# Score-maximum pairs between the projections: visits of three slots, with the two row halves out of step

## The chip, the core and the metric

One core of a Trainium2 chip runs the whole kernel. The metric is the device time of one execution in microseconds (us); the median of three executions of the kernel before is 1766.52 us.

## What is computed

A transformer block with adaptive layer norm over 2048 rows of 512 elements, in float32. The part that matters here is the attention with 32 heads of 16 elements, and in it the softmax, whose row maximum the kernel finds ahead of the attention itself.

```python
q, k, v = qkv[0], qkv[1], qkv[2]            # from (h @ wqkv), 32 heads, Dh = 16
scores = jnp.einsum("bhqd,bhkd->bhqk", q, k) * scale
p = _softmax(scores, axis=-1)
o = jnp.einsum("bhqk,bhkd->bhqd", p, v)
...
x = x + ga * _A_ref(h, A_wqkv, A_wo)        # attention
h = _layernorm(x, axis=-1) * (1 + cb) + sb
x = x + gb * _B_ref(h, B_w1, B_b1, B_w2, B_b2)   # two-layer network with gelu
```

## The kernel before

The kernel writes the order of each engine's instructions out by hand (`manual_schedule`, L56): what the program emits first is what an engine executes first. Waits between engines follow from the tiles. PSUM has eight banks of 128 x 512 floats, and the kernel hands them out in fixed rings (L69 to L88): a product takes the next bank of its ring, and TensorE (PE) can write a bank only when the engine that reads the former product from it is done.

The program has four stages: norms and first projections (to about 92 us), the remaining projections (to about 301 us), the attention over 32 units of 4 heads and 512 query rows, and the network. This case is about the second.

*The projections.* `items` (L580) lists 34 of them: ten blocks of v and 24 of q and k. Each is a sum of twelve 128x128 by 128x512 products in one bank (`mm3`, L294: three terms, since each operand is split in a high and a low part), read by one copy on ScalarE (ACT; L316 or L361). `mm3` takes a list `fill` of functions and calls them spread evenly between its twelve products. With five, they fall behind products 3, 5, 8, 10 and 12.

*The pairs.* The softmax needs a bound on each row's maximum. For nine of the 32 units (`FRONT`, L36; `NU1` = 9) it is found in this stage, between the projections' products. The keys are held as sums and differences of two column blocks (`kpm`, built at L325 to L350), so that max(x, y) = (x + y)/2 + |x - y|/2: one product gives the differences ("V") and one the sums ("U"). `pair_slot` (L434) does one slot, which is V or U of pair n, for both row halves: a = 0 uses rows 0 to 47 of the array, a = 1 rows 64 to 111. A V slot ends in two absolute values on ACT, from PSUM to the SBUF tile `cp` (L454, six buffers). A U slot ends in two operations on VectorE (DVE; L458), each of which adds the product to its `cp` and takes the minimum along the row (signs are turned) into one column of `mxs`. Each is followed by a small read of the accumulator. There are 144 pairs, so 288 slots and 576 products, ACT operations and DVE operations in sum. When a unit is complete, `max_rows` (L462) reduces its columns on DVE, splits them on GpSimd (POOL), and one or two projections later transposes them on DVE and stores them by four DMAs; this goes through the list `todo`, of which each projection takes one entry (L636 to L638). `load_qm` (L392), called in V of every unit's third pair, loads the next unit's queries by six DMAs on SyncE's queue (SP).

*The order.* `slots` (L582 to L585) is V0, V1, V2, U0, V3, U1, ..., so that U of a pair stands five slots behind its V. `visit` (L589) does the next `VISIT` = 2 of them. From the seventh projection on (`FILL0` = 6), `fill` holds five visits, six in every seventh projection (L632): 144 in 28 projections. For this stage the pair products have a ring of six banks and the projections one of two (L572). After the stage the rings are dealt anew (L647), the keys of two more groups are loaded, and the attention begins.

Of the kernel before, what the change touches and what calls it, by code (L numbers as in the profile page):

```python
# [7 lines left out]
F32 = mybir.dt.float32  # L8
FR = mybir.dt.float32r
BF = mybir.dt.bfloat16  # L10
AF = mybir.ActivationFunctionType
ALU = mybir.AluOpType
# [4 lines left out]
P = 128  # L17
# [7 lines left out]
NB = 4  # L25
TB = S // NB
# [5 lines left out]
KR = 3 * DH  # L32
# [3 lines left out]
FRONT = (0, 1, 2, 3, 4, 5, 8, 6, 7, 9)  # L36
NU1 = len(FRONT) - 1
FILL0 = 6
VISIT = 2
OP0 = 1  # L40
OPN = 4
NWARM = 22
# [10 lines left out]
def block_kernel(ctx: ExitStack, tc: tile.TileContext, x, wqkv, wo, w1, b1, w2, b2, c, w_mod, out):  # L53
    nc = tc.nc
    te, ve, ac, gp, sy = nc.tensor, nc.vector, nc.scalar, nc.gpsimd, nc.sync
    ctx.enter_context(tc.manual_schedule())  # L56

    def pool(name, bufs=1, **kw):
        cm = tc.tile_pool(name=name, bufs=bufs, **kw)
        return cm, cm.__enter__()  # L60

    def close(cm):
        cm.__exit__(None, None, None)
# [10 lines left out]
    def ring(n):  # L74
        b = rings[n].pop(0)
        rings[n].append(b)
        return psum[b].tile([P, TB], F32, tag="b", name=n)

    def bank_mx():
        return ring("mx")  # L80

    def bank():
        return ring("sc")
# [35 lines left out]
    tcm, tpool = pool("tpool", bufs=2, side="right")  # L119
# [33 lines left out]
    def load_w(k):  # L153
        if k < 4:
            raw = tpool.tile([P, 2, KC, P], F32, tag="wraw", name="wraw")
            for w in (1, 0):
                sy.dma_start(raw[:, w], wq_r[:, :, w * D + k * P : w * D + (k + 1) * P])
        else:
            raw = vraw
            for i in range(KC):  # L160
                sy.dma_start(raw[:, i], wq_r[:, i, 2 * D :])
        raws[k] = raw
# [108 lines left out]
    def ln1(b):  # L271

        tiles = [x_tile(b, t) for t in range(4)]
        mv, rs = ln_stats(tiles)

        def rows():
            for t in range(4):
                ve.tensor_scalar(tiles[t], tiles[t], mv[:, t, 0:1], rs[:, t : t + 1],
                                 op0=ALU.subtract, op1=ALU.mult)
            return tiles  # L280

        return rows
# [84 lines left out]
    kst, kpm, qst, qmx = {}, {}, {}, {}  # L367
# [6 lines left out]
    def build_k(dst, src, g, t0=0, t1=S, parts=(0, 1, 2)):  # L374
        for i in parts:
            part = (0, 0, 1)[i]
            for a in range(2):
                r0 = a * 64 + i * DH
                sy.dma_start(dst[r0 : r0 + DH, :, t0:t1].bitcast(F32), heads(src, g, part, a, t0, t1))

    def load_k(g, tile):
        kst[g] = tile
        build_k(tile, qk_d[1][g // 2], g)

    def build_q(u, dst):
        g, qb = divmod(u, NB)
        for i, part in enumerate((0, 1, 0)):
            for a in range(2):
                r0 = a * 64 + i * DH
                sy.dma_start(dst[r0 : r0 + DH].bitcast(F32), heads(qk_d[0][g // 2], g, part, a, qb * TB, (qb + 1) * TB))  # L390

    def load_qm(u):  # L392

        qmx[u] = qmpool.tile([P, 2, TB], FR, tag="qmx", name="qmx", bufs=2)
        build_q(u, qmx[u])

    def load_q(u):

        qst[u] = qpool.tile([P, 2, TB], FR, tag="qst", name="qst", bufs=2)
        build_q(u, qst[u])  # L400
        if u in have:
            load_max(u)
# [9 lines left out]
    def one_rows(k):  # L412
        for a in range(2):
            r0 = a * 64 + KR
            sy.dma_start(k[r0 : r0 + 2].bitcast(F32), one_d[:, None, :].to_broadcast([2, 2, S]))

    mxs, left, vabs = {}, {}, {}
# [13 lines left out]
        ve.tensor_reduce(mxs[u][:, p, a, qc, kr : kr + 1], ps, axis=AX.X, op=ALU.max, negate=True)  # L431
        left[u] -= 1

    def pair_slot(kind, n):  # L434


        v, i = divmod(n, 16)
        u = FRONT[v]
        if u not in left:
            mxs[u] = small.tile([P, 2, 2, 4, 2], F32, tag="mxf", name="mxf")  # L440
            left[u] = 16
        r, p, qc = i // 8, (i // 4) % 2, i % 4
        t0 = (2 * r + (kind == "V")) * TB
        pss = [bank_mx() for _ in range(2)]
        for a, ps in enumerate(pss):
            rows = slice(a * 64, a * 64 + KR)
            te.matmul(ps, qmx[u][rows, p, qc * P : (qc + 1) * P], kpm[u // NB][rows, p, t0 : t0 + TB],  # L447
                      start=True, stop=True)
        if kind == "V" and i == 2:
            load_qm(FRONT[v + 1])  # L450
        if kind == "V":
            for a, ps in enumerate(pss):
                vabs[n, a] = tpool.tile([P, TB], F32, tag="cp", name="cp", bufs=6)
                ac.activation(vabs[n, a], ps, AF.Abs)  # L454
            return []
        for a, ps in enumerate(pss):
            v = vabs.pop((n, a))
            ve.tensor_tensor_reduce(v, ps, v, -0.5, 3.0e38, ALU.add, ALU.min, mxs[u][:, p, a, qc, r : r + 1])  # L458
        left[u] -= 1
        return [] if left[u] else [max_rows(u)]  # L460

    def max_rows(u):  # L462

        mn = small.tile([P, 2, 2, 4], F32, tag="mn", name="mn")
        ve.tensor_reduce(mn, mxs.pop(u), axis=AX.X, op=ALU.min)  # L465


        m2 = small.tile([P, 2, 16], FR, tag="m2", name="m2")
        mt = small.tile([P, 32], F32, tag="mt", name="mt")
        mf = mn.rearrange("p b a c -> p (b a c)")  # L470
        gp.tensor_copy(m2[:, 0], mf)  # L471
        gp.tensor_tensor(m2[:, 1], mf, m2[:, 0].bitcast(F32), op=ALU.subtract)

        def rest():
            ve.transpose(mt, m2.rearrange("p s j -> p (s j)").bitcast(F32))
            for b in range(4):
                q0 = b * 32
                sy.dma_start(m_d[u][:, :, q0 : q0 + 32].rearrange("s j q -> (s j) q"), mt[q0 : q0 + 32])
            have.add(u)
            if u in qst:  # L480
                load_max(u)

        return rest
# [30 lines left out]
    ps = bank()  # L514
# [10 lines left out]
    rest = lambda: None  # L525
# [8 lines left out]
    for b in range(NB):  # L534
# [7 lines left out]
        if b + 1 < NB:  # L542
            rows = ln1(b + 1)
# [32 lines left out]
    def load_v(g):  # L576
        vg[g] = vgpool.tile([P, NKC, VG], F32, tag="vg", name="vg")
        sy.dma_start(vg[g], v_d[:, :, g])

    items = [(None, b, t) for b, t in vitems] + [(k, b, w) for k in range(1, 4) for b in range(NB) for w in (1, 0)]  # L580
    nv = len(vitems)
    slots = [("V", 0), ("V", 1)]  # L582
    for n in range(2, 16 * NU1):
        slots += [("V", n), ("U", n - 2)]
    slots += [("U", 16 * NU1 - n) for n in (2, 1)]  # L585
    led, todo = 0, []
    new = []

    def visit():  # L589
        nonlocal led  # L590
        for sl in slots[led : led + VISIT]:
            new.extend(pair_slot(*sl))
        led += VISIT

    for n, (k, b, w) in enumerate(items):
        if n == 1:
            close(acm)
            st[0] = sy
        if n < 3:
            build_k(kts[0], kpm_d[0], 0, 2 * TB, S, (n,))  # L600
        if n == 8:
            build_k(kts[1], kpm_d[0], 1)
            for t in kts:
                one_rows(t)
        if n == nv + 1:
            close(vwcm)
            kqcm, kqpool = pool("kqpool")
            kq = [kqpool.tile([P, 2, S], FR, name="kq0")]
            one_rows(kq[0])
            vgcm, vgpool = pool("vgpool", bufs=2)  # L610
            qcm, qpool = pool("qpool")
        if n == nv + 2:
            load_k(0, kq[0])
        if n == nv + 10:
            kpm[2] = kts[0]
            build_k(kts[0], kpm_d[1], 2)
        if n == nv + 15:
            load_v(0)
        if n == nv + 19:
            load_k(2, kts[0])  # L620
        if n == nv + 18:
            load_q(0)
        if n == nv + 20:
            load_q(1)
        if k and b == 1 and w and k < 3:
            split_w(k + 1)
            if k + 2 < 4:
                load_w(k + 2)
        new = []
        fill = [rest]  # L630
        if n >= FILL0:
            fill = [lambda rest=rest: (rest(), visit())] + [visit] * (4 + (n % 7 == 0))  # L632
        if n == len(items) - 1:
            fill += [lambda: None] * 2
        rest = proj_qk(b, k, w, fill) if k else proj_v(b, w, fill)
        for f in todo[:1]:  # L636
            f()
        todo = todo[1:] + new  # L638
    rest()
    while led < len(slots):  # L640
        new = []
        visit()
        todo += new
# [219 lines left out]
    for s in range(NS):  # L863
        u, kc = divmod(s, NKC)
# [3 lines left out]
        new = []  # L868
# [156 lines left out]
```

## Time and profile before

| | |
|---|---|
| median of three executions | 1766.52 us (1766.45 to 1767.83) |
| the profiled execution, its own time | 1765.35 us |
| its span, first to last instruction | 1763.6 us |
| granted TensorE clock, mean | 0.998 |
| first pair product | 92.2 us |
| last pair product starts | 300.0 us |
| first product of the attention | 301.20 us |

The profile is of one execution. Times of the timeline count from the first instruction. A row of the timeline gives the start, the length, the engine, the line of the kernel, the operation, what it writes from what, and how many such instructions in a row were joined; "PEld" is TensorE loading weights, which has its own row and can overlap the products. A bracket at its end gives the engine's idle time before it and what ended it. The length of a product holds the time in the array's pipeline, so that the distance between the starts of two bursts tells more than the busy time.

### The profile page before, as it was taken

The page shows a single profiled execution, that of the slowest core. Times are in us where ns is not written, and L with a number is a line of the kernel's source. Part 1 is how long each engine was busy: PE and PEld are TensorE (multiplying, and loading weights), DVE is VectorE, ACT ScalarE, POOL GpSimd, SP SyncE. Part 2 cuts the span into 40 slices and gives each one's busy share as a digit, 9 for nine tenths or more (in the row PEclk, how much of TensorE's full clock was granted, in tenths as well). Part 3 has the DMA queues.
Part 4 walks back from the last instruction along what each step waited for, and adds up shares of the span by engine and source line. Part 5 has one row for each costly group of instructions (what it writes and reads, how often), then busy time and mean ns, then how long its engine had stood idle before and what let it go on. Part 6 is the DMA issues. An engine that isn't in the chain of part 4 may idle for free.

```text
span 1763.6 us, 29164 instructions
## 1 busy us (share of the span) xinstructions
PE 1748.7 (99%) x10554; PEld 901.1 (51%) x10554; DVE 1404.5 (80%) x2553; ACT 1355.8 (77%) x2580; POOL 320.1 (18%) x347
## 2 busy tenths in 40 slices
PE   8999999999999999999999999999999999999998
PEld 6755555344343443343343343343433478788887
DVE  6579999898888888888888888888886286838453
ACT  3478888999999999999999999999999732213222
POOL 3204422010000000000000000000003154636462
PEclk9999999999999999999999999999999999999999
DMA  8767636811500411411410101101013064423341
GB/s 277 250 141 163 151 115 130 130 37 29 87 23 23 82 27 23 74 36 23 74 35 24 38 25 33 38 23 36 23 60 104 22 195 131 126 78 114 102 120 48
DMA packets 124100, 144.17 MB, mean 82 GB/s; under 512 B 38930, under 2 KB 72722, under 8 KB 122004
## 3 DMA queue, kind: packets, MB, share of 16 engines
q1 hardware_dynamic: 120644, 135.55, 30.9%
q10 hardware_dynamic: 3312, 6.76, 1.0%
q8 instruction: 83, 1.36, 0.3%
q14 instruction: 61, 0.50, 0.1%
HBM read 106.37 MB, written 35.87 MB: 81 GB/s over the span
## 4 chain that ended last, share of the span: by engine, by line
PE 93%; DVE 3%; DMA 1%; issue 1%; POOL 1%; SPq 0%; ACT 0%; ACTq 0%; DVEq 0%; POOLq 0%
PE pv L693 29%; PE mx L429 19%; PE sc L300 16%; PE sc L860 13%; PE mx L447 6%; PE mx L924 5%; PE pv L924 2%; PE sc L800 1%; PE mx L800 1%; DMA wmod<-in_w_mod_dram 1%; DVE glo L907 0%; POOL w2l L731 0%; DMA rb<-rden 0%; PE sc L257 0%; DVE mxs L431 0%
## 5 line engine op out<-in xcount | busy, mean ns | idle before, releaser
L861 ACT ACTIVATE p<-sc 128x512 f32<-128x512 f32 x2048 | 1054.8, 615 | 39.4 <-PE sc L860 13.4
L431 DVE TENSOR_REDUCE mxs<-mx 128x1 f32<-128x512 f32 x1472 | 927.5, 684 | 112.9 <-PE sc L860 76.6
L693 PE MATMUL pv<-p,vg 128*32 128x512 f32 x4096 | 546.0, 605 | 0.0
L860 PE MATMUL sc<-qst,kq 50*128 50x512 f32 x1024 | 284.1, 435 | 0.0
L860 PE MATMUL sc<-qst,kt 50*128 50x512 f32 x1024 | 282.3, 431 | 0.0
L429 PE MATMUL mx<-kq,qmx 48*128 48x512 f32 x768 | 262.1, 428 | 0.2
L429 PE MATMUL mx<-kt,qmx 48*128 48x512 f32 x704 | 240.3, 428 | 0.1
L429 PEld LDWEIGHTS mx<-kq,qmx 48*128 48x128 f32 x768 | 122.6, 184 | 228.5 <-DVE mxs L431 209.2
L903 ACT ACTIVATE g<-sc,b_c 128x512 f32<-128x512 f32 x56 | 38.6, 690 | 237.2 <-PE sc L300 233.1
L429 PEld LDWEIGHTS mx<-kt,qmx 48*128 48x128 f32 x704 | 113.3, 184 | 208.8 <-DVE mxs L431 191.1
L458 DVE CUSTOM_DVE_ANT_0 cp<-mx,cp 128x512 f32<-128x512 f32 x288 | 187.2, 688 | 36.3 <-PE mx L447 31.3
L471 POOL CAST m<-mn 128x16 fp32r<-128x16 f32 x32 | 6.3, 197 | 1026.0 <-DVE mn L465 1026.0
L454 ACT ACTIVATE cp<-mx 128x512 f32<-128x512 f32 x288 | 156.3, 597 | 38.8 <-PE mx L447 38.4
L693 PEld LDWEIGHTS pv<-p,vg 128*32 128x32 f32 x4096 | 81.1, 108 | 180.7 <-issue 169.3
L860 PEld LDWEIGHTS sc<-qst,kq 50*128 50x128 f32 x1024 | 125.5, 185 | 32.1 <-ACT p L861 23.6
L907 DVE TENSOR_TENSOR glo<-g,ghi 128x512 fp32r<-128x512 f32 x56 | 60.1, 1073 | 94.8 <-ACT ghi L906 94.8
L860 PEld LDWEIGHTS sc<-qst,kt 50*128 50x128 f32 x1024 | 125.5, 185 | 10.1 <-ACT p L861 3.1
L447 PE MATMUL mx<-kt,qmx 48*128 48x512 f32 x576 | 113.4, 455 | 0.0
L729 POOL TENSOR_TENSOR w1l<-w1r,w1h 128x512 fp32r<-128x512 f32 x56 | 76.8, 1372 | 152.7 <-DVE w1h L728 130.5
L447 PEld LDWEIGHTS mx<-kt,qmx 48*128 48x128 f32 x576 | 58.3, 184 | 56.4 <-issue 33.4
L300 PE MATMUL sc<-hThi,w 128*128 128x512 f32 x256 | 84.0, 436 | 2.2 <-DVE hThi L263 2.2
L731 POOL TENSOR_TENSOR w2l<-w2r,w2h 128x512 fp32r<-128x512 f32 x56 | 81.1, 1448 | 6.6 <-DVE w2h L730 6.2
(158 smaller groups left out, 1671.4 us busy)
## 6 DMA issues: line engine op xcount, KB each, us to landing
w1r<-in_B_w_dram SPq DMA_DIRECT2D x56, 256.0 KB
w2r<-in_B_w_dram SPq DMA_DIRECT2D x56, 256.0 KB
qk<-parts SPq DMA_DIRECT2D x25, 512.0 KB
qmx<-qk SPq DMA_DIRECT2D x192, 64.0 KB
qst<-qk SPq DMA_DIRECT2D x192, 64.0 KB
wmod<-in_w_mod_dram SPq DMA_DIRECT2D x6, 1024.0 KB
kq<-qk SPq DMA_DIRECT2D x24, 256.0 KB
kt<-qk SPq DMA_DIRECT2D x24, 256.0 KB
```

The costliest lines, as they stand in the source:

```text
L300: te.matmul(ps, p, q, start=i == 0, stop=i == len(terms) - 1)
L429: te.matmul(ps, qmx[u][rows, p, qc * P : (qc + 1) * P], kst[u // NB][rows, p, kr * TB : (kr + 1) * TB], start=True, stop=True)
L431: ve.tensor_reduce(mxs[u][:, p, a, qc, kr : kr + 1], ps, axis=AX.X, op=ALU.max, negate=True)
L447: te.matmul(ps, qmx[u][rows, p, qc * P : (qc + 1) * P], kpm[u // NB][rows, p, t0 : t0 + TB], start=True, stop=True)
L454: ac.activation(vabs[n, a], ps, AF.Abs)
L458: ve.tensor_tensor_reduce(v, ps, v, -0.5, 3.0e38, ALU.add, ALU.min, mxs[u][:, p, a, qc, r : r + 1])
L693: te.matmul(cur_pv[0][32 * j : 32 * (j + 1)], vg[g][:, kc, j * VW : j * VW + 32], pt.pop((s, j)), start=kc == 0, stop=kc == NKC - 1)
L729: gp.tensor_tensor(alo, a, ahi.bitcast(F32), op=ALU.subtract)
L731: gp.tensor_tensor(blo, b, bhi.bitcast(F32), op=ALU.subtract)
L860: te.matmul(ps, k[r0 : r0 + KX, p, kc * P : (kc + 1) * P], q[r0 : r0 + KX, p], start=True, stop=True)
L861: ac.activation(pb, ps, AF.Exp, scale=SCALE)
L924: te.matmul(acc[qb][t], p[:, sl], q, start=f == 0 and n == 0, stop=f == NF - 1 and n == 2)
```

## The change

`VISIT` becomes 3. The list of slots is first written for one row half (`half`: V0, nothing, V1, U0, V2, U1, ..., nothing, U143), 290 entries. U of a pair stands three entries behind its V. The other half (a = 1) follows the same list one entry later. So in a slot one half does V while the other does U, and each slot gives one operation to ACT and one to DVE; at three of the 291 slots only one half has work. `half_slot` is `pair_slot` for one half. The products, the operations on ACT and DVE, the buffers and the rings are the same. The 97 visits are spread over the 28 projections, three in 15 of them and four in 13; in the last projection two empty entries are added to `fill`, as before.

```diff
-VISIT = 2
+VISIT = 3
...
-    def pair_slot(kind, n):
+    def half_slot(kind, n, a):
...
-            left[u] = 16
+            left[u] = 32
         r, p, qc = i // 8, (i // 4) % 2, i % 4
         t0 = (2 * r + (kind == "V")) * TB
-        pss = [bank_mx() for _ in range(2)]
-        for a, ps in enumerate(pss):
-            rows = slice(a * 64, a * 64 + KR)
-            te.matmul(ps, qmx[u][rows, p, qc * P : (qc + 1) * P], kpm[u // NB][rows, p, t0 : t0 + TB],
-                      start=True, stop=True)
-        if kind == "V" and i == 2:
-            load_qm(FRONT[v + 1])
+        rows = slice(a * 64, a * 64 + KR)
+        ps = bank_mx()
+        te.matmul(ps, qmx[u][rows, p, qc * P : (qc + 1) * P], kpm[u // NB][rows, p, t0 : t0 + TB],
+                  start=True, stop=True)
         if kind == "V":
-            for a, ps in enumerate(pss):
-                vabs[n, a] = tpool.tile([P, TB], F32, tag="cp", name="cp", bufs=6)
-                ac.activation(vabs[n, a], ps, AF.Abs)
+            if i == 2 and a == 0:
+                load_qm(FRONT[v + 1])
+            vabs[n, a] = tpool.tile([P, TB], F32, tag="cp", name="cp", bufs=6)
+            ac.activation(vabs[n, a], ps, AF.Abs)
             return []
-        for a, ps in enumerate(pss):
-            v = vabs.pop((n, a))
-            ve.tensor_tensor_reduce(v, ps, v, -0.5, 3.0e38, ALU.add, ALU.min, mxs[u][:, p, a, qc, r : r + 1])
+        v = vabs.pop((n, a))
+        ve.tensor_tensor_reduce(v, ps, v, -0.5, 3.0e38, ALU.add, ALU.min, mxs[u][:, p, a, qc, r : r + 1])
         left[u] -= 1
...
-    slots = [("V", 0), ("V", 1)]
-    for n in range(2, 16 * NU1):
-        slots += [("V", n), ("U", n - 2)]
-    slots += [("U", 16 * NU1 - n) for n in (2, 1)]
+
+    half = [("V", 0), None]
+    for n in range(1, 16 * NU1):
+        half += [("V", n), ("U", n - 1)]
+    half += [None, ("U", 16 * NU1 - 1)]
+    slots = list(zip(half + [None], [None] + half))
+    visits = -(-len(slots) // VISIT)
...
         for sl in slots[led : led + VISIT]:
-            new.extend(pair_slot(*sl))
+            for a in range(2):
+                if sl[a]:
+                    new.extend(half_slot(*sl[a], a))
...
-            fill = [lambda rest=rest: (rest(), visit())] + [visit] * (4 + (n % 7 == 0))
+            m, nm = n - FILL0, len(items) - FILL0
+            fill = [lambda rest=rest: (rest(), visit())] + [visit] * (visits * (m + 1) // nm - visits * m // nm - 1)
```

## The prediction

> **What bounds the kernel now.** I read first the page's totals and its chain of waits, then the stage that the change touches.
>
> ```profile
> span 1763.6 us, 29164 instructions
> PE 1748.7 (99%) x10554; PEld 901.1 (51%) x10554; DVE 1404.5 (80%) x2553; ACT 1355.8 (77%) x2580; POOL 320.1 (18%) x347
> ...
> PE 93%; DVE 3%; DMA 1%; issue 1%; POOL 1%; SPq 0%; ACT 0%; ACTq 0%; DVEq 0%; POOLq 0%
> PE pv L693 29%; PE mx L429 19%; PE sc L300 16%; PE sc L860 13%; PE mx L447 6%; PE mx L924 5%; PE pv L924 2%; PE sc L800 1%; PE mx L800 1%; DMA wmod<-in_w_mod_dram 1%; DVE glo L907 0%; POOL w2l L731 0%; DMA rb<-rden 0%; PE sc L257 0%; DVE mxs L431 0%
> ```
>
> PE carries 93% of the chain, and the pair products (L447) and projections (L300) are on it. So a microsecond that PE saves in their stage should be saved at the end, unless another engine takes over there. The stage's limits, from the line's own record, the first instruction of the attention behind it, and busy times by stretch (PE, weight loads, DVE, ACT, POOL, clock, DMA share, GB/s):
>
> ```profile
> L447 PE MATMUL mx<-kt,qmx x576: 383/492/503, 92.2 to 300.0; 48*128 48x512 f32 x192
> ```
>
> ```profile
> 301.20 0.72 PE L860 MATMUL sc<-qst,kq 50*128 50x512 f32 x3
> ```
>
> ```profile
> 150.00:200.00 50.00, 50.00 (x219) 26.35 (x218) 45.71 (x143) 40.92 (x77) 24.52 (x29) 1.00 0.49 162
> 200.00:250.00 50.00, 50.00 (x221) 26.24 (x220) 45.50 (x143) 40.35 (x77) 15.70 (x21) 1.00 0.56 131
> ```
>
> The stage lasts from 92.2 to 301.2: 209.0 us. PE is called busy throughout, DVE for 91% (45.5 of 50), ACT for 81%. A PE "busy" at 100% says little, since the record of a matmul holds its waiting too; what it does with the time is in the starts of its bursts (start, length, engine, line, count):
>
> ```profile
> 84.90 1.09 PE L300 MATMUL sc<-wv,hTlo 128*128 128x512 f32 x4
> 85.84 2.03 PE L300 MATMUL sc<-wv,hThi 128*128 128x512 f32 x8
> ...
> 182.47 0.73 PE L447 MATMUL mx<-kt,qmx 48*128 48x512 f32 x4
> 183.00 1.09 ACT L454 ACTIVATE cp<-mx 128x512 f32<-128x512 f32 x2
> 183.13 0.73 PE L300 MATMUL sc<-hThi,w 128*128 128x512 f32 x2
> 183.24 0.69 DVE L458 CUSTOM_DVE_ANT_0 cp<-mx,cp 128x512 f32<-128x512 f32 x1 [0.26 <-PE mx L447]
> 183.79 0.84 PE L447 MATMUL mx<-kt,qmx 48*128 48x512 f32 x4
> 183.85 0.09 DVE L458 DVE_READ_ACCUMULATOR2_ANT mxf<- 128x1 f32 x1
> 183.85 0.69 DVE L458 CUSTOM_DVE_ANT_0 cp<-mx,cp 128x512 f32<-128x512 f32 x1
> 184.32 1.09 ACT L454 ACTIVATE cp<-mx 128x512 f32<-128x512 f32 x2 [0.23 <-PE mx L447]
> 184.56 0.97 PE L300 MATMUL sc<-hThi,w 128*128 128x512 f32 x3
> 185.46 0.73 PE L447 MATMUL mx<-kt,qmx 48*128 48x512 f32 x4
> 186.12 0.73 PE L300 MATMUL sc<-hTlo,w 128*128 128x512 f32 x2
> ```
>
> Projections alone start every 0.235 us (84.90 to 85.84, four of them). Between pair products, a burst of two takes 0.66 (183.13 to 183.79) and one of three 0.89 (184.56 to 185.45). So a burst of n costs 0.19 + 0.235 n: each change between the 128-row products and the 48-row pairs costs 0.19 beyond the matmuls. The four pair products of a visit take 0.66 too (182.47 to 183.13): the two of a slot, on different row halves, run together, and a slot counts as one position. One visit in two takes 0.77 (183.79 to 184.56): 0.11 of waiting.
>
> By this count the stage now has 144 visits of two positions (144 x 0.66 = 95.0) and, inside the window, 144 projection bursts with 333 matmuls (144 x 0.19 + 333 x 0.235 = 105.6): 200.6. The other 8.4 of the 209.0 are about 76 waits of 0.11. ACT explains them: in the visit at 182.47 its two Abs end at 183.00 + 1.09 = 184.09, and the second position of the visit at 183.79, which takes over their two banks, would start at 183.79 + 0.33 = 184.12 with its weight load ahead of that.
>
> **The change, part by part.** *Fewer, longer visits.* 291 slots make 97 visits of three, three in 15 of the 28 projections and four in 13. 47 visits fewer save 47 x 2 x 0.19 = 17.9. Three half slots at the ends stand alone, so 291 positions replace 288 (0.7 more). A burst of three positions was never run here; I take 0.19 + 3 x 0.235 = 0.895, as for three projections; its upper bound is 1.00, with the 0.11 above. Counted out: 97 x 0.895 = 86.8 for the pairs; the gaps inside the window are 45 of four projections (1.13 each, 50.9), 48 of three (0.895, 43.0), and 4 of two in the last projection (0.66, 2.6). PE unhindered: 183.3, plus 0.2 since the first visit comes one matmul later.
>
> *Halves out of step.* Each slot now gives one Abs to ACT and one sum-and-minimum to DVE, instead of two to one of them by turns. The number of operations is unchanged. I read their prices from the groups of this stretch (busy time, then the mean ns of one) and, in the timeline, from two runs without a gap:
>
> ```profile
> L458 DVE CUSTOM_DVE_ANT_0 cp<-mx,cp 128x512 f32<-128x512 f32 x286 | 186.0, 688 | 36.3 <-PE mx L447 31.3
> L454 ACT ACTIVATE cp<-mx 128x512 f32<-128x512 f32 x288 | 156.3, 597 | 38.8 <-PE mx L447 38.4
> ...
> L316 ACT ACTIVATE raw<-sc 128x512 f32<-128x512 f32 x23 | 13.9, 604 | 0.0
> ...
> L475 DVE STREAM_TRANSPOSE mt<-m 128x32 f32<-128x32 f32 x8 | 1.6, 206 | 0.0
> ...
> L465 DVE TENSOR_REDUCE mn<-mxf 128x16 f32<-128x32 f32 x8 | 1.5, 186 | 0.3
> ```
>
> ```profile
> 92.75 4.09 ACT L454 ACTIVATE cp<-mx 128x512 f32<-128x512 f32 x8 [0.46 <-PE mx L447]
> ...
> 300.92 0.69 DVE L458 CUSTOM_DVE_ANT_0 cp<-mx,cp 128x512 f32<-128x512 f32 x1
> ...
> 301.53 0.69 DVE L458 CUSTOM_DVE_ANT_0 cp<-mx,cp 128x512 f32<-128x512 f32 x1
> ```
>
> Back to back, one DVE operation follows the other after 0.61 (300.92 to 301.53), though each lasts 0.69; an Abs after 0.51 (4.09 / 8). A visit of three thus needs 1.83 of DVE and 1.53 of ACT, against a PE period of 0.895 + 0.895 = 1.79 (gap of three) or 2.025 (gap of four). **This is where the gain meets its limit**: in the denser projections DVE is slower than PE.
>
> *The banks.* Six matmuls use up the ring of six, so every bank is wanted again exactly one visit later, and PE, which issues in order, stops at the first that isn't free. From a visit's start at 0: the first position's data are read from 0.53 (ACT in the rows: 182.47 to 183.00), DVE's third operation ends its accumulator read at 0.53 + 3 x 0.61 + 0.08 = 2.44. The next visit's third position starts 0.895 - 0.33 = 0.57 after that visit. With a gap of four it wants its bank at 2.025 + 0.57 = 2.60: free in time. With a gap of three at 1.79 + 0.57 = 2.36: 0.08 too early, and a late load costs the 0.11 besides, so a period of up to 1.98. DVE working without a pause gives 1.83; after a late visit the next is nearer to that. I take the middle, 1.91. In the last projection, with gaps of two, I take DVE's 1.83.
>
> Sum: 48 x 1.91 + 45 x 2.025 + 4 x 1.83 = 91.7 + 91.1 + 7.3 = 190.1. DVE's nine mn and mt jobs (0.19 + 0.21 each, 3.5 in all) sit beside PE work in the loose half, on the path in the tight half: 1.8. With the 0.2 above: 192.1 instead of 209.0, **16.9 us less**.
>
> *Cost nothing:* ACT's raw copy (0.60 once a projection) follows the three Abs of a visit and ends at 0.53 + 1.53 + 0.60 = 2.66; the next three end at 2.66 + 1.53 = 4.19, where with a gap of three their third bank is wanted at 1.79 + 2.36 = 4.15. DVE's operations end later than that anyway; uncovered, it is 0.04 + 0.11 in each of the 13 denser projections, 2.0, kept for the range. The waits behind the operations: U of a pair falls on the bank of its own V, six matmuls back, and V's cp buffer comes from the U whose bank it takes, so the bank waits of PE already cover both. The loads:
>
> ```profile
> 265.58 1.71 SPq L478 DMA_DIRECT2D m<-mt  x4
> 267.33 2.76 SPq L379 DMA_DIRECT2D kt<-qk  x6
> ...
> 286.72 3.88 SPq L390 DMA_DIRECT2D qmx<-qk  x6
> ```
>
> load_qm comes 28 slots before its first use: 28 x 0.73 = 20 us now (209.0 / 288), 28 x 0.66 = 18 then. The tail is the tight place: kt waits on SP behind the m stores at the end of the projection whose raw copy is the sixth from last, 36 us before the attention, and the qmx load for the attention is issued only at 286.72. After the change five projections remain from there: two with three visits (3 x 2.025 = 6.08), two with four (4 x 1.91 = 7.64) and the last (some 8): 35, nearly as long, so this chain isn't squeezed. Nothing behind the stage is altered; it moves forward whole.
>
> **The rivals.** *PE unhindered (1741):* if the third position's bank is free in time, because DVE starts sooner than 0.53 after a visit, the stage takes 183.5, 25.5 less. Against it: 1.83 of DVE in a period of 1.79, 52 times.
>
> *DVE sets the pace (1760):* if alternating waits keep the operations from following at 0.61, each costs 0.61 + 0.08 = 0.69: 288 x 0.69 + 3.5 = 202.2, 6.8 us less than before. For it: the custom operation's own record is 0.69. Against it: 300.92 to 301.53, and 183.24 to 183.85. The Trainium skill, in "TensorEngine Tiling (Array Packing)", section "PSUM Bottleneck", speaks for this one: packing the array speeds up the matmuls but not the emptying of PSUM, which then may become the bottleneck. By that rule alone the stage would stay at DVE's sum, as in this rival; the trace agrees as far as DVE's 91%, but leaves it 9%.
>
> *Six banks in one visit (slower, 1773 or more):* if the last release of a visit is needed earlier than in its third position, PE and DVE take turns. Needed at the second position, the period is 2.44 + 0.11 - 0.33 = 2.22, 97 x 2.22 = 215, 6 us more than before; at the first, 2.55 and 247, 38 us more. It decides at a mean period of 209 / 97 = 2.15. For it: no bank is spare any more. Against it: the bank order, worked out above, and weight loads that each wait for their own bank.
>
> *No change (1766.5):* if the stage's end hung on loads or POOL and not on PE. Against it: the attention's first matmul starts at the end of a PE burst, and its data's chain has slack.
>
> **How the numbers follow.** The profiled execution took 1765.35 (its span 1763.6); the median of three is 1766.52. 16.9 off that is **1749.6**. Chances: forecast 0.56 (its own range 1744 to 1757), unhindered 0.10, DVE's pace 0.22, no change 0.04, slower 0.08. Less than 0.2% (3.5 us) can't be told from no change. Faster 0.88, same 0.04, slower 0.08. The range 1743 to 1762 holds the forecast with the raw copy's 2.0, and DVE's pace with 2 us of start and end; it leaves out the slower rival, no change and the unhindered end.
>
> **What would show it.** Right: pair bursts "x6" of 0.9 to 1.0, 97 of them, the stage's end near 284.6, DVE above 95% busy in the stage, and PE's idle time before L447 ended by DVE's mxf rather than by "issue" in the projections with four visits, and hardly in those with three. The step on the switches is wrong if x6 bursts take over 1.1 in the loose projections; that on DVE, if operations without a wait follow at 0.69; that on banks, if the first or second weight load of a visit waits for DVE. The forecast is wrong if the attention begins after 294, or if it begins near 285 and the span doesn't shrink with it.

## The result and the profile after

The changed kernel takes 1751.04 us (median of four, 1749.52 to 1751.21) against 1766.49 (median of four, 1766.41 to 1767.83): a ratio of 0.9906, interval 0.9894 to 0.9918. That is 15.45 us less; 16.9 were forecast, and 1749.6 for the time.

The page of the changed kernel, its totals and the chain by engine:

```profile
span 1749.3 us, 28886 instructions
PE 1732.7 (99%) x10554; PEld 900.7 (51%) x10554; DVE 1396.8 (80%) x2553; ACT 1350.3 (77%) x2580; POOL 320.2 (18%) x347
...
PE 93%; DVE 3%; DMA 1%; issue 1%; POOL 1%; SPq 0%; ACT 0%; ACTq 0%; DVEq 0%; POOLq 0%
```

The same instructions are busy, 16 us less on PE, and the chain has the same shares: nothing new became the bound. The record of the pair products (now line 446) and, from the timeline, the first product of the attention:

```profile
L446 PE MATMUL mx<-kt,qmx x576: 383/425/502, 93.5 to 285.4; 48*128 48x512 f32 x192
```

```profile
286.83 0.50 PE L863 MATMUL sc<-qst,kq 50*128 50x512 f32 x2
```

The stage lasts from 93.45 to 286.83, 193.4 us instead of 209.0: **15.6 less**. Behind it 1462.4 us are left in both (1763.6 - 301.2 and 1749.3 - 286.8): all of it arrives at the end. Ahead of the stage the changed profile is 1.2 late, 0.2 of it because the first visit stands one product later; the rest arises in the first 24 us, where PE waits for the inputs. In the nine profiles of this study in which the visits start in the seventh projection, that start lies anywhere from 91.8 to 95.2, and what lies behind the stage lasts from 1460.9 to 1464.8 in all ten profiles, so that its equality here is partly chance. So below I compare the lengths of the stage, and single times only roughly; a time without an interval is that of one execution.

Busy times by stretch (columns as before):

```profile
150.00:200.00 50.00, 50.00 (x241) 28.51 (x238) 48.07 (x157) 42.46 (x82) 26.49 (x31) 1.00 0.61 171
200.00:250.00 50.00, 50.00 (x239) 28.30 (x236) 48.17 (x156) 42.51 (x82) 14.53 (x20) 1.00 0.53 142
```

DVE went from 91% to 96%, ACT from 81% to 85%. In the timeline, first a projection with three visits, then one with four:

```profile
184.37 1.20 PE L300 MATMUL sc<-hThi,w 128*128 128x512 f32 x4
185.50 0.98 PE L446 MATMUL mx<-kt,qmx 48*128 48x512 f32 x6
185.98 0.19 PEld L446 LDWEIGHTS mx<-kt,qmx 48*128 48x128 f32 x2 [0.19 <-DVE mxf L455]
186.41 1.19 PE L300 MATMUL sc<-hTlo,w 128*128 128x512 f32 x4
187.53 1.00 PE L446 MATMUL mx<-kt,qmx 48*128 48x512 f32 x6
...
196.63 0.96 PE L300 MATMUL sc<-hThi,w 128*128 128x512 f32 x3
196.78 0.69 DVE L455 CUSTOM_DVE_ANT_0 cp<-mx,cp 128x512 f32<-128x512 f32 x1
197.39 0.69 DVE L455 CUSTOM_DVE_ANT_0 cp<-mx,cp 128x512 f32<-128x512 f32 x1
197.53 1.11 PE L446 MATMUL mx<-kt,qmx 48*128 48x512 f32 x6
198.00 0.08 DVE L455 DVE_READ_ACCUMULATOR2_ANT mxf<- 128x1 f32 x1
198.14 0.19 PEld L446 LDWEIGHTS mx<-kt,qmx 48*128 48x128 f32 x2 [0.32 <-DVE mxf L455]
198.57 0.72 PE L300 MATMUL sc<-hThi,w 128*128 128x512 f32 x2
```

With gaps of four a visit takes 0.91 (185.50 to 186.41). With gaps of three it takes 1.04 (197.53 to 198.57): the weight loads of the third position, the last two of the six, start at 198.14, just after DVE's accumulator read of the visit before (198.00 + 0.08). That is the wait that the prediction priced, and it isn't the only such visit. Of the two weight loads of a third position, one takes over a bank that DVE empties; in all 48 visits behind a gap of three, this load starts 0.05 us after the end of DVE's accumulator read. Behind gaps of four, 39 of 43 follow within 0.1 too, but there they are late by little.

Over the whole stage, from the starts of the bursts (the gap is the number of projection products ahead of a visit; a visit lasts from its first product to the next projection product; without a wait that is 0.66 for two positions and 0.895 for three; the first visit and a few at the end of the stage are left out):

```
kernel              stage us  visits behind a gap of: 2          3          4
before               209.0    97 x 0.74   45 x 0.67   -
changed              193.4     3 x 1.28   48 x 1.06   44 x 0.93
halves out, two      202.1    97 x 0.66   43 x 0.66   -
halves in, three     219.0     4 x 1.53   44 x 1.36   47 x 1.20
one DVE op more      198.9     3 x 1.41   48 x 1.17   44 x 0.94
one ACT op more      193.3     3 x 1.28   48 x 1.07   44 x 0.93
from the fourth      197.3     3 x 1.26   12 x 1.06   80 x 0.93
gaps evened          194.9     -          55 x 1.12   40 x 0.90
```

### The profile page after: what moved, and what is told of

It is laid out like the page before. It is cut to its first block, busy times and chain, and to the rows that moved or that the text cites. A ratio compares the mean times of both kernels' runs of the same rounds, so it can differ in the third digit from the quotient of the medians.

```text
span 1749.3 us, 28886 instructions
## 1 busy us (share of the span) xinstructions
PE 1732.7 (99%) x10554; PEld 900.7 (51%) x10554; DVE 1396.8 (80%) x2553; ACT 1350.3 (77%) x2580; POOL 320.2 (18%) x347
## 4 chain that ended last, share of the span: by engine, by line
PE 93%; DVE 3%; DMA 1%; issue 1%; POOL 1%; SPq 0%; ACT 0%; ACTq 0%; DVEq 0%; POOLq 0%
PE pv L696 29%; PE mx L429 20%; PE sc L300 15%; PE sc L863 13%; PE mx L927 5%; PE mx L446 5%; PE pv L927 2%; PE sc L803 1%; PE mx L803 1%; DVE glo L910 0%; DMA wmod<-in_w_mod_dram 0%; POOL w2l L734 0%; DMA rb<-rden 0%; PE sc L257 0%; PE mx L257 0%
## 5 line engine op out<-in xcount | busy, mean ns | idle before, releaser
L429 PE MATMUL mx<-kt,qmx 48*128 48x512 f32 x704 | 240.0, 428 | 0.0
L429 PEld LDWEIGHTS mx<-kt,qmx 48*128 48x128 f32 x704 | 113.4, 184 | 208.4 <-DVE mxs L431 190.6
L455 DVE CUSTOM_DVE_ANT_0 cp<-mx,cp 128x512 f32<-128x512 f32 x288 | 182.5, 687 | 25.9 <-PE mx L446 23.2
L452 ACT ACTIVATE cp<-mx 128x512 f32<-128x512 f32 x288 | 151.6, 604 | 27.9 <-PE mx L446 27.0
L910 DVE TENSOR_TENSOR glo<-g,ghi 128x512 fp32r<-128x512 f32 x56 | 58.6, 1046 | 96.2 <-ACT ghi L909 96.2
L446 PE MATMUL mx<-kt,qmx 48*128 48x512 f32 x576 | 103.9, 442 | 0.1
L446 PEld LDWEIGHTS mx<-kt,qmx 48*128 48x128 f32 x576 | 54.6, 184 | 52.7 <-DVE mxf L455 26.4
L300 PE MATMUL sc<-hThi,w 128*128 128x512 f32 x256 | 77.7, 421 | 3.1 <-DVE hThi L263 3.1
```

Source lines behind the costliest of these rows:

```text
L300: te.matmul(ps, p, q, start=i == 0, stop=i == len(terms) - 1)
L429: te.matmul(ps, qmx[u][rows, p, qc * P : (qc + 1) * P], kst[u // NB][rows, p, kr * TB : (kr + 1) * TB], start=True, stop=True)
```

## The experiments

### The two halves of the change, each alone

The first keeps visits of two slots in the changed kernel:

```diff
-VISIT = 3
+VISIT = 2
```

> The changed kernel with visits of two slots (146 visits): the halves out of step alone. Theory (switches cost 0.19 each, and the waits of 0.11 of the kernel before come from ACT doing two Abs at once): no waits are left, 146 x 0.66 for the pairs and 146 x 0.19 + 333 x 0.235 for the projections, so the stage takes 202 to 204 us instead of 193.4 (changed) and 209.0 (before), and the time is 1760 to 1762. Rival 1, only the number of visits counts: the stage stays at 209 to 210 as before, 1767. Rival 2, only the step between the halves counts: 193, 1751.

It took 1759.76 us (ratio to before 0.9956, interval 0.9939 to 0.9972), just below the expected range, and its stage 202.1. In its timeline:

```profile
182.18 0.97 PE L300 MATMUL sc<-hThi,w 128*128 128x512 f32 x3
183.08 0.73 PE L446 MATMUL mx<-kt,qmx 48*128 48x512 f32 x4
183.74 0.73 PE L300 MATMUL sc<-hTlo,w 128*128 128x512 f32 x2
184.40 0.73 PE L446 MATMUL mx<-kt,qmx 48*128 48x512 f32 x4
185.06 0.73 PE L300 MATMUL sc<-hTlo,w 128*128 128x512 f32 x2
```

Every visit takes 0.66 (183.08 to 183.74, 184.40 to 185.06), behind gaps of three and of two alike: the waits of the kernel before are gone, and with them 6.9 us, with two visits more than before. Out-of-step halves are worth that much alone. The second puts visits of three into the kernel before, whose halves go in step:

```diff
-VISIT = 2
+VISIT = 3
...
+    visits = -(-len(slots) // VISIT)
...
-            fill = [lambda rest=rest: (rest(), visit())] + [visit] * (4 + (n % 7 == 0))
+            m, nm = n - FILL0, len(items) - FILL0
+            fill = [lambda rest=rest: (rest(), visit())] + [visit] * (visits * (m + 1) // nm - visits * m // nm - 1)
```

> The kernel before with visits of three slots (96 visits) in its own order, both halves in step: visits of V U V and U V U by turns. Theory (with six banks in one visit, DVE and ACT must share the work evenly): four operations of one engine come in one visit, DVE's last release falls at 0.53 + 4 x 0.61 + 0.08 = 3.05 or at 2.6, and the third position waits 0.4 and 0.8 by turns; mean period about 2.3, the stage 216 to 228 us, the time 1774 to 1786, slower than before. Rival, the number of visits alone counts: 193, 1751.

It took 1777.37 us, the stage 219.0: 10 us slower than before, although it changes between the products as seldom as the changed kernel does. Its timeline:

```profile
180.96 1.09 PE L447 MATMUL mx<-kt,qmx 48*128 48x512 f32 x6
181.98 0.96 PE L300 MATMUL sc<-hTlo,w 128*128 128x512 f32 x3
182.28 3.66 ACT L454 ACTIVATE cp<-mx 128x512 f32<-128x512 f32 x6 [0.78 <-DVE mxf L458]
182.87 1.70 PE L447 MATMUL mx<-kt,qmx 48*128 48x512 f32 x6
184.08 0.18 PEld L447 LDWEIGHTS mx<-kt,qmx 48*128 48x128 f32 x1 [0.35 <-DVE mxf L458]
184.51 1.20 PE L300 MATMUL sc<-hThi,w 128*128 128x512 f32 x4
```

One visit takes 1.02 (180.96 to 181.98), the next 1.64 (182.87 to 184.51): in it positions wait for DVE and ACT, which by turns get four operations in one visit. ACT itself stood idle 0.78 for DVE, since here an Abs also waits for a cp buffer. The view of waits counts these (total us, times, longest):

```profile
ACT cp L454 <- DVE mxf L458: 31.1, 42, 1.1
```

There is no such entry in the kernel before, nor in the changed one. How much of the loss comes from DVE and ACT getting four operations in one visit, and how much from the six cp buffers, this run doesn't tell; none was made with more buffers. Either way, the two halves of the change aren't a sum: alone they are worth -6.9 and +10.1, together -15.6.

### Which engine sets the pace in the dense projections

One unused operation more at the end of each visit, on DVE and, in another kernel with the same tile, on ACT (both lines are shown in one diff):

```diff
+    extra = const.tile([P, 64], F32, name="extra")
...
+        ve.tensor_reduce(extra[:, :1], ident, axis=AX.X, op=ALU.max)
         led += VISIT
...
+        ac.activation(extra, ident[:, :64], AF.Copy)
         led += VISIT
```

> The changed kernel with one operation more on DVE at the end of each visit (a maximum over 128 columns of a constant tile, about 0.2 us, its result unused). Theory (DVE's 3 x 0.61 set the pace in the projections with four visits, and have some 0.15 spare in those with three): the 52 visits behind gaps of three or two get longer by 0.17 to 0.21, the 45 behind gaps of four by 0 to 0.05: 9 to 13 us more, 1760 to 1764. Rival, ACT's three Abs or the latency of a bank set the pace: 0 to 3 us more, 1751 to 1754.

> The changed kernel with one operation more on ACT at the end of each visit (a copy of 64 columns of a constant tile, about 0.2 us, its result unused). Theory (DVE sets the pace, ACT has 0.2 spare at the third bank): 0 to 4 us more, 1751 to 1755. Rival, ACT sets the pace: 52 visits get longer by 0.15 to 0.2, 8 to 11 us more, 1759 to 1762.

On ACT it cost nothing: 1750.33 us, the stage 193.3. Its row in the groups (97 of 275 ns, 26.7 us of work that don't show in the time):

```profile
L596 ACT ACTIVATE extra<-ident 128x64 f32<-128x64 f32 x97 | 26.7, 275 | 0.0
```

On DVE the stage grew by 5.5 to 198.9: 0.10 in each visit behind a gap of three, 0.004 behind a gap of four. The time of 1760.00 lies in the expected range, but only 5.5 of its 9.0 more come from the stage (its profile begins the stage 1.7 late and has 1.7 more behind it), so the expected 9 to 13 were too many. DVE's own timeline says why:

```profile
186.14 0.68 DVE L456 CUSTOM_DVE_ANT_0 cp<-mx,cp 128x512 f32<-128x512 f32 x1
186.75 0.69 DVE L456 CUSTOM_DVE_ANT_0 cp<-mx,cp 128x512 f32<-128x512 f32 x1
187.36 0.69 DVE L456 CUSTOM_DVE_ANT_0 cp<-mx,cp 128x512 f32<-128x512 f32 x1
187.97 0.28 DVE L596 TENSOR_REDUCE extra<-ident 128x1 f32<-128x128 f32 x1
188.18 0.69 DVE L456 CUSTOM_DVE_ANT_0 cp<-mx,cp 128x512 f32<-128x512 f32 x1
```

With the extra operation DVE works without a pause, 2.04 a visit (186.14 to 188.18), and the period behind gaps of three is 0.895 + 1.17 = 2.06: now it is DVE's throughput. Without it the period is 1.96 and DVE's work 1.83: 0.13 of the 0.21 that the operation takes had been pause, the few mn and mt jobs aside. So in the changed kernel DVE's latency, the way from a visit's first products to the third release, sets the pace and not its throughput.

### Throughput or latency: even gaps

If DVE's throughput counted, it would help to alternate gaps of three and four, 1.90 on the average:

```diff
-            fill = [lambda rest=rest: (rest(), visit())] + [visit] * (visits * (m + 1) // nm - visits * m // nm - 1)
-        if n == len(items) - 1:
-            fill += [lambda: None] * 2
+            t = 12 * nm - 4
+            done = [min(visits, visits * (12 * m + i) // t) for i in range(13)]
+            fill = [lambda k=done[i + 1] - done[i], r=rest if not i else None: (r and r(), [visit() for _ in range(k)])
+                    for i in range(12)]
```

> The changed kernel with its 97 visits spread evenly over the products of all projections, so that gaps of three and four products alternate, instead of whole projections with gaps of three and others with gaps of four. Theory (a visit behind a gap of three is late because DVE's last release takes 2.44 us from the start of the visit before, whatever came ahead of that): some 50 gaps of three with 0.17 to 0.24 each as now, the stage 192 to 196 us, the time 1750 to 1754. Rival, DVE's throughput over several visits sets the pace (mean period 1.90 against 1.83): hardly any wait, the stage 184 to 188, the time 1742 to 1746.

It took 1753.42 us, the stage 194.9, so the rival fell. In the timeline a visit behind three projection products and one behind four:

```profile
179.80 0.97 PE L300 MATMUL sc<-hThi,w 128*128 128x512 f32 x3
180.70 1.25 PE L446 MATMUL mx<-kt,qmx 48*128 48x512 f32 x6
181.88 0.50 PE L300 MATMUL sc<-hThi,w 128*128 128x512 f32 x1
182.22 0.86 PE L300 MATMUL sc<-hTlo,w 128*128 128x512 f32 x3
183.00 0.99 PE L446 MATMUL mx<-kt,qmx 48*128 48x512 f32 x6
183.93 0.50 PE L300 MATMUL sc<-hTlo,w 128*128 128x512 f32 x1
```

1.18 and 0.93; over all, 55 x 1.12 and 40 x 0.90. A visit behind a gap of four is late by nothing. Of the 55 behind a gap of three, the 40 whose visit before stands behind a gap of four take 1.18 on the average (1.12 to 1.39), late by 0.28 (0.17 to 0.24 was expected), although DVE had stood idle for 0.22 on the average just before its work on the visit before. The 14 that directly follow another gap of three take 0.94: the visit before them is itself late, and its length gives DVE the time. What counts is the distance from one visit's start to the next visit's third position, and not the mean period.

### The length of a visit

```diff
-VISIT = 3
+VISIT = 1
```

> The changed kernel with visits of one slot (291 visits). Theory (each change between pair products and projection products costs 0.19): 291 x 0.425 + 291 x 0.19 + 332 x 0.235 = 257, the stage takes 254 to 258 us, the time is 1811 to 1816. Rival, the cost of a change is a constant of weight loads that overlap when bursts are short: the stage below 240, the time below 1798.

1818.67 us, the stage 259.3, both a little over the expected ranges (a position takes 0.430 instead of 0.425, 1.5 in all), and no overlap of short bursts. The timeline:

```profile
200.53 0.50 PE L446 MATMUL mx<-kt,qmx 48*128 48x512 f32 x2
200.97 0.49 PE L300 MATMUL sc<-hTlo,w 128*128 128x512 f32 x1
201.39 0.50 PE L446 MATMUL mx<-kt,qmx 48*128 48x512 f32 x2
201.82 0.49 PE L300 MATMUL sc<-hTlo,w 128*128 128x512 f32 x1
```

A burst of one position or of one product takes 0.42 to 0.44, which is 0.19 or 0.20 + 0.235. So the price of a change holds for bursts of one to four. The other way, visits of four on the ring of six:

```diff
-VISIT = 3
+VISIT = 4
```

> The changed kernel with visits of four slots (73 visits) on the same ring of six banks. Theory (a visit can't hold more slots than half the banks): the fourth position wants the first one's banks 0.8 after the visit's start, and DVE gives them back at 0.53 + 0.61 + 0.08 with 0.11 for the late load, 1.33 to 1.39: 73 x (1.13 + 0.55) + 332 x 0.235 + 73 x 0.19 = 215, the stage takes 208 to 220 us, the time is 1766 to 1778. Rival, fewer changes always win: 174 of PE, or DVE's 180, the time 1732 to 1740.

1775.49 us, the stage 216.5, slower than before. Its timeline:

```profile
181.43 0.96 PE L446 MATMUL mx<-kt,qmx 48*128 48x512 f32 x6
182.61 0.32 PEld L446 LDWEIGHTS mx<-kt,qmx 48*128 48x128 f32 x2 [0.65 <-ACT cp L452]
182.62 0.63 PE L446 MATMUL mx<-kt,qmx 48*128 48x512 f32 x2 [0.22 <-ACT cp L452]
183.18 1.18 PE L300 MATMUL sc<-hTlo,w 128*128 128x512 f32 x4
184.28 0.96 PE L446 MATMUL mx<-kt,qmx 48*128 48x512 f32 x6
```

The fourth position can't start before the first one's banks are free, 1.19 after the visit's start (181.43 to 182.62); a visit takes 1.75 instead of 1.13. In all 48 visits behind a gap of four, both weight loads of the fourth position start 0.05 after the release of their banks, one by ACT and one by DVE. Six banks hold three positions; a longer visit waits inside itself.

### A faster version

If only gaps of three cost something, the visits should have more products between them. They start three projections earlier:

```diff
-FILL0 = 6
+FILL0 = 3
```

> The changed kernel with the visits starting three projections earlier (in the fourth instead of the seventh): 97 visits over 31 projections, so that 27 have three visits and only 4 have four. Theory (waits of 0.17 behind a gap of three projection products, 0.04 behind a gap of four): 36 gaps change from three to four, 36 x 0.13 = 4.7 us less, 1745 to 1748. Rival, the waits belong to every visit whatever its gap: 1750 to 1752. Second rival, the keys' sums and differences, loaded during these projections, come too late for an earlier start: 1752 or more, with a wait of TensorE for a load in the first visits.

It took **1747.54 us** (median of four, 1746.95 to 1748.33; ratio to before 0.9894, interval 0.9878 to 0.9911), 3.5 less than the changed kernel. Its stage holds 36 more projection products (36 x 0.235 = 8.5), and 197.3 - 8.5 = 188.8 is 4.6 less than 193.4, as expected (4.7). Not all of it arrives in the time, since a wait ahead of the first visit lies outside this length. The second rival shows there, once:

```profile
86.98 1.02 PE L446 MATMUL mx<-kt,qmx 48*128 48x512 f32 x3 [0.93 <-DMA kt<-kpm]
```

The first visit waited 0.93 for the keys' load. A still earlier start, which was not run, should have little to win: 12 gaps of three are left, 12 x 0.13 = 1.6 by the same count.

## Why the prediction was right

*The price of a change between products, 0.19.* Right. 97 projection bursts took 96.2 in the changed kernel (96.5 counted), and bursts of one position, which were never run before, keep the price.

*A burst of three positions, 0.895.* Right: 0.90 behind gaps of four with even gaps.

*Why the kernel before waited.* Right. The 8.4 us of waits are gone when the halves go out of step; that run alone doesn't tell ACT from DVE, which then also gets its operations one by one. The trace of the kernel before does. In 94 of 96 visits behind a gap of two, the weight load of the fourth product starts 0.05 after the second Abs of the visit before has ended. In the 62 of them that take about 0.77 it starts 0.33 to 0.39 after the visit's start, in the others at most 0.25. For the visit at 183.79, where the prediction has this Abs end at 184.09, the load is:

```profile
184.14 0.18 PEld L447 LDWEIGHTS mx<-kt,qmx 48*128 48x128 f32 x1
```

*The third position, with gaps of three 0.12 on the average, with gaps of four nothing.* The place and the engine were right, the sizes a little small: 0.17 and 0.04. The latency itself was right: DVE's third release comes 2.45 at the least and 2.51 on the average after the start of a visit that a gap of three follows, against 2.44. But the step took the middle between DVE without pause (1.83) and a fresh start (1.98); measured is 1.96, near the latter. By terms: 48 x 0.05 = 2.4 and 44 x 0.037 = 1.6 more; the mn and mt jobs, priced at 1.8 by themselves, are contained in these waits; and the first and the last visit, in whose six slots (not three) only one half has work, hold three products each and take 0.66 instead of 0.895, 0.5 less. That leaves 1.7, and the stage is 1.5 longer than the 191.9 forecast beside the first visit's 0.2. That the total is so near is partly luck, since 4.0 too little for the waits and 2.3 too much elsewhere offset each other.

*Raw copies, cp buffers and loads at no cost.* Right: another 0.28 of ACT work a visit changes nothing, and the tail behind the stage is as long as before.

*The rivals.* PE unhindered would have been 183.5 for the stage, DVE at 0.69 each 202.2; 193.4 lies between, and operations that follow at 0.61 through a whole visit (186.14 to 187.97, with more work on DVE) refute the second. The Trainium skill's "TensorEngine Tiling (Array Packing)", section "PSUM Bottleneck", is borne out in a weaker form than in that rival: emptying PSUM does limit the denser gaps, by when it gives back a bank rather than by its sum (288 x 0.61 + 3.5 = 179). The section speaks of a fourfold speedup; here two products run together. The slower rival's point, a release needed before the third position, wasn't reached here, but in-step halves and visits of four, which wait at other positions too, are both slower than the kernel before.

*Three signs didn't come as written.* The stage's end was put near 284.6 (the sum gives 301.2 - 16.9 = 284.3) and came at 286.8; 1.0 lies ahead of the stage. Of "x6" bursts there are 95 instead of 97, and 62 are longer than 1.0, among them 47 of the 48 behind gaps of three. And the idle time before PE's weight loads was to be ended by DVE in the projections with four visits, and hardly in those with three. The view of waits doesn't separate them; in the changed kernel:

```profile
PEld mx L446 <- DVE mxf L455: 26.4, 84, 0.4
...
PEld mx L446 <- ACT cp L452: 17.1, 47, 0.4
PEld mx L446 <- issue: 4.7, 13, 0.4
```

131 of these 144 entries are put down to an engine. In the kernel before, which waited less, 90 went to "issue":

```profile
PEld mx L447 <- issue: 32.7, 90, 0.4
```

Yet 32.7 / 90 = 0.36 and 17.1 / 47 = 0.36: most entries are the idle time that follows any change of products. In the changed kernel all 97 bursts have one of 0.36 or 0.37 on the average ahead of their first load, under any of the names. Such a name says whose signal came last, not that it was late. Sorted by their place in the burst, the entries do separate: ahead of a third position's loads, 33 of the 48 visits behind gaps of three have one that DVE ended, and 11 of the 44 behind gaps of four. So the sign was right in kind, and its "hardly" too strong.

## What to carry to other kernels

Where two kinds of products alternate on PE, count the changes: here each costs as much as most of a product. How seldom one can change is set by the banks: a burst as long as the ring paid here with the work of the engines that empty it spread evenly through the burst, and lost with the halves in step; and then what counts is when the last bank comes back, measured from the start of that burst to its next use. Test both parts of such a change together, since a longer burst alone can lose what the pair gains.

## What the runs showed of the hardware

A record on DVE can be longer than the engine's turn: 0.69 recorded, 0.61 from one start to the next over whole visits, and a maximum over 128 columns 0.28 recorded, 0.21 (187.97 to 188.18) taken. A product's wait for its bank showed in its weight load, which started 0.05 us after the reader's last record ended (48 of 48 visits behind gaps of three, 94 of 96 in the kernel before). And the start of the stage, which no edit but the first visit's place touches, moved by over 3 us from one execution to another, with the arrival of the first inputs: more than some of the effects studied, so that the stage's own length had to be the measure.
